# A product with stationary weights and 512 tokens moving, its sums turned in squares of 32 on VectorE

## The chip, the core and the metric

The kernel runs on one core of a Trainium2 chip. The metric is device time in microseconds of one execution. The engines of a core work side by side, each in the order of its own instruction list: PE (TensorE, matmuls; PEld is its weight load), DVE (VectorE), ACT (ScalarE), POOL (GpSimd); SP (SyncE) issues the DMAs. In a matmul one operand is stationary (loaded with LDWEIGHTS, 128x128) and the other moves past it column by column; the sums land in PSUM, eight banks of 128 partitions x 512 numbers. Compute engines read and write SBUF, 128 partitions.

## The reference

Chunked attention (batch 4, 8 heads, 768 tokens, head size 64) gives 3072 tokens x 512. Two feed-forward blocks follow:

```python
def _moe_ref(x, w1, w2, w3, w_out):
    h = np.maximum(np.maximum(x @ w1, x @ w2), x @ w3)      # 512 -> 768
    return (h @ w_out).astype(np.float32)                   # 768 -> 512

def _moe2_ref(x, w_in, w_out):
    h = x @ w_in                                            # 512 -> 2048
    g = np.where(h >= 1, h, np.where(h <= -1, 0.0, (h + 1) ** 2 / 4.0))
    return (g @ w_out).astype(np.float32)                   # 2048 -> 512
```

The change is in the last product, g @ w_out.

## The kernel before

All numbers are float32. A product is made of three fast matmuls: each operand is split into a rounded high half (float32r, made by ACT) and the rest (low half = value - high half, made by DVE or POOL), and high x high, high x low and low x high are added up in PSUM (`mm3`).

The first 500 us hold attention and the first feed-forward block, in 24 units of 128 tokens. Meanwhile the weights of the second block are prepared and put into DRAM in combinations (`cd` for w_in; `rd` and `td` for w_out). The second block then runs in three pairs of token blocks (2 x 512 tokens). A pair has two stages, and each of them multiplies 2 x 2 block matrices with seven block products in place of eight, in Winograd's form.

The stage on w_in, `pair_slot` for n = 0 to 7. Each n makes seven products of 128 features x 512 tokens, 6 matmuls of 512 columns each; the combined w_in is stationary and the combinations of x (`mat`, tiles t and b) move. Products go to the eight PSUM banks in turn. DVE adds them up to the four blocks h11, h12, h21 and h22 of the activations (feature x token); `g_start` (two ACT instructions) and `g_end` (one of DVE) apply the gate; `difference` (POOL) then replaces h21 by h11 - h21. Between products, `fill` splits the next w_in tile (`split_c`, ACT and POOL) or begins to split h for the next stage.

The stage on w_out, `pair_l4`: 56 steps, seven products k = 0 to 6 of eight steps. A step takes one tile of h (128 features x 512 tokens), split into hi and lo, and its w_out tile `w` (128 features x 256 outputs, `w[:, 0]` high, `w[:, 1]` low). For each 128 of the 512 tokens, three matmuls hold 128x128 of hi or lo and move the 256 columns of w: twelve matmuls a step into four banks (lines 820 to 822). In the same step `split_h(i + 4)` issues the split of the tile four steps ahead: ACT the high half (L746), DVE or POOL the low half (L748), DVE where the step number is in `ON_V`. The halves lie in nine buffers (`hb`) used in turn, so a low half's buffer is free when the step four before its own has been multiplied.

`evict` adds a finished product to the sums of the output blocks, one of the four banks (128 tokens x 256 outputs) in each of the next product's first four steps: two copies by ACT at first, otherwise adds by DVE, from PSUM into `outs`. A finished block is stored in rows of 256 numbers (`store_out`, L768).

`L4_STEPS` puts further work into the steps: L.. loads a half of a streamed w_out combination (`load_t`, into a buffer of `mat`; L30 is the first half for k = 3), S.. makes a combination of h blocks (`sum_h`, DVE, L764; two tiles at once, 1024 columns, or two times 512), X is the last `difference`, A to D load the four tiles of the next pair (`prep`, L646), T1 to T4 are their differences (DVE, L651), b11, t1 and so on split these (ACT L656, DVE L657), and c splits the first w_in tiles. The third pair has no successor and leaves A to t4 out. The order of every engine's list is the order of this code; nothing reorders it. SP waits at each DMA for what that one needs, and all later DMAs wait behind.

Of the kernel before, what the change touches and what calls it, by code (L numbers as in the profile page):

```python
# [19 lines left out]
P = 128  # L20
# [45 lines left out]
def attention_then_two_mlps(ctx, tc, q, k, v, mem_k, mem_v, w1, w2, w3, w_mid, w_in, w_out, out):  # L66
# [570 lines left out]
    SPOT = {"A": ("h11", 0), "B": ("h11", 1), "D": ("h11", 2), "C": ("h11", 3), "E": ("h21", 0)}  # L637
# [53 lines left out]
    def pair_slot(p, n, mid, fill):  # L691
# [3 lines left out]
        c21, c11, c12 = fb[0], fb[4], fb[5]  # L695
        h11, h12, h21, h22 = [h_tile(q, n) for q in ("h11", "h12", "h21", "h22")]
# [58 lines left out]
    def load_t(k, half):  # L755
        i = (2, 0, 1, 3)[k - 3]
# [3 lines left out]
    def sum_h(k, g):  # L760
        (o, a, b), op = {3: (("h11", "h22", "h11"), ALU.add), 5: (("h22", "h22", "h21"), ALU.subtract),
# [40 lines left out]

    outs = []

    def pair_l4(p, steps):

        for i in range(7 * HF):
            k, f = divmod(i, HF)
            if f == 0:
                done = cur.get("l4")  # L810
                cur["l4"] = acc4 = [next_bank() for _ in range(TB // P)]
# [5 lines left out]
            for t in range(TB // P):  # L817
                c = slice(t * P, (t + 1) * P)
                o = acc4[t][:, 0:HK]
                nc.tensor.matmul(o, hi[:, c], w[:, 0], start=f == 0, stop=False)  # L820
                nc.tensor.matmul(o, hi[:, c], w[:, 1], start=False, stop=False)  # L821
                nc.tensor.matmul(o, lo[:, c], w[:, 0], start=False, stop=f == HF - 1)  # L822
# [268 lines left out]
```

## Time and profile before

| | us |
|---|---|
| median of 3 runs | 1019.1 (1018.61 to 1019.78) |
| profiled execution | 1016.97 |
| its span, first to last instruction | 1015.2 |
| stages on w_in, pairs 2 and 3 | 77.50, 77.37 |
| stages on w_out, pairs 1, 2, 3 | 85.30, 84.75, 82.67 |

The rows below are from the profiled execution; times are from the start of its span. A stage is counted from the start of its first matmul to that of the next stage, the last one to the end of its last matmul. Rows of instructions name line, engine, operation and out<-in tiles without buffer numbers: hb is a half of a split, h a block of activations or a tile of the next pair, f a sum or a gate buffer, d, b and t weights of w_out or combinations of x. The granted clock of PE is 1.00 in all these stages, the higher of its two levels, 2.4 GHz.

### The profile page before, as it was taken

The numbers are of one execution on the slowest core, as the hardware profiler recorded it, in microseconds if no ns is written. First come the engines' busy times: TensorE is split into PE (matmuls) and PEld (weight loads), VectorE is DVE, ScalarE is ACT, GpSimd is POOL, SyncE is SP. The second block draws the span as 40 slices with busy tenths as digits, with TensorE's granted clock in tenths as the row PEclk, the third lists the DMA queues.
The fourth block names the chain that finished last, engine by engine and source line by source line (L and its number), as shares of the span: only waits on it lengthen the run. The fifth ranks groups of instructions, "written<-read, shape, count | busy, mean of one in ns | idle before, by whom it ended". The sixth has DMA issues, their size and how long they took to land.

```text
span 1015.2 us, 21316 instructions
## 1 busy us (share of the span) xinstructions
PE 983.1 (97%) x8262; PEld 832.7 (82%) x8262; DVE 725.5 (71%) x1096; ACT 521.9 (51%) x926; POOL 454.1 (45%) x368
## 2 busy tenths in 40 slices
PE   8999889999999999999999999999999999999998
PEld 6777677878788778788878889988889998888998
DVE  4699935567665776662337779898778988777974
ACT  5676434443234323322448775456786445786542
POOL 0024312222221011111647768487787667776754
PEclk9999999999999999999999999999999999999999
DMA  7857536667767576414323346313338033334421
GB/s 167 219 157 204 144 118 187 156 161 219 181 167 190 157 179 198 141 66 165 120 63 128 90 122 242 123 45 114 94 93 307 28 135 99 95 91 158 168 64 63
DMA packets 201781, 142.57 MB, mean 140 GB/s; under 512 B 128208, under 2 KB 169168, under 8 KB 201680
## 3 DMA queue, kind: packets, MB, share of 16 engines
q1 hardware_dynamic: 201680, 141.21, 47.8%
q8 instruction: 65, 1.06, 0.5%
q14 instruction: 36, 0.29, 0.1%
HBM read 109.71 MB, written 31.46 MB: 139 GB/s over the span
## 4 chain that ended last, share of the span: by engine, by line
PE 66%; DVE 12%; issue 6%; DMA 5%; ACT 4%; POOL 3%; SPq 3%; DVEq 0%; POOLq 0%; ACTq 0%
PE bank L502 14%; PE bank L503 14%; PE bank L504 14%; PE bank L822 6%; PE bank L820 6%; PE bank L821 6%; POOL hb L616 3%; SPq L846 2%; DVE c L145 2%; DVE c L150 1%; ACT f L678 1%; PE bank L373 1%; DVE c L142 1%; DMA st<-in_moe_w_dram 1%; PE bank L415 1%
## 5 line engine op out<-in xcount | busy, mean ns | idle before, releaser
L748 POOL TENSOR_TENSOR hb<-h,hb 128x512 fp32r<-128x512 f32 x96 | 165.6, 1737 | 78.2 <-PE bank L822 52.6
L502 PE MATMUL bank<-xh,hi 128*128 128x512 f32 x432 | 175.5, 406 | 1.2 <-ACT xh L443 0.7
L521 POOL TENSOR_TENSOR hl_a<-t,hh_a 128x512 fp32r<-128x512 f32 x34 | 47.5, 1396 | 281.6 <-ACT hh_a L519 222.1
L504 PE MATMUL bank<-xh,lo 128*128 128x512 f32 x432 | 169.3, 392 | 1.9 <-POOL lo L204 1.9
L503 PE MATMUL bank<-xl,hi 128*128 128x512 f32 x432 | 169.5, 392 | 0.3 <-DVE xl L447 0.2
L746 ACT CAST hb<-h 128x512 fp32r<-128x512 f32 x168 | 101.5, 621 | 90.4 <-PE bank L822 89.8
L537 DVE TENSOR_TENSOR t<-bank,t 128x512 f32<-128x512 f32 x72 | 49.4, 687 | 90.6 <-PE bank L504 90.3
L616 POOL TENSOR_TENSOR hb<-ra,hb 128x256 fp32r<-128x256 f32 x96 | 87.9, 933 | 28.8 <-ACT hb L615 23.3
L748 DVE TENSOR_TENSOR hb<-h,hb 128x512 fp32r<-128x512 f32 x72 | 87.0, 1218 | 18.1 <-PE bank L822 9.9
L504 PEld LDWEIGHTS bank<-xh,lo 128*128 128x128 f32 x432 | 81.4, 189 | 20.5 <-POOL lo L204 2.7
L502 PEld LDWEIGHTS bank<-xh,hi 128*128 128x128 f32 x432 | 81.6, 189 | 19.1 <-DVE t L537 1.0
L503 PEld LDWEIGHTS bank<-xl,hi 128*128 128x128 f32 x432 | 81.7, 189 | 16.1 <-DVE xl L447 1.0
L678 ACT ACTIVATE f<-h 128x512 f32<-128x512 f32 x96 | 60.8, 633 | 57.5 <-DVE h L713 35.2
L822 PE MATMUL bank<-d,hb 128*128 128x256 f32 x288 | 82.5, 287 | 3.6 <-POOL hb L748 2.8
L685 DVE SCALAR_TENSOR_TENSOR h<-f,h 128x512 f32<-128x512 f32 x96 | 78.8, 821 | 6.3 <-ACT f L679 6.0
L820 PE MATMUL bank<-d,hb 128*128 128x256 f32 x288 | 81.2, 282 | 0.0
L821 PE MATMUL bank<-d,hb 128*128 128x256 f32 x288 | 81.1, 282 | 0.0
L502 PE MATMUL bank<-t,hb 128*128 128x512 f32 x192 | 75.4, 393 | 0.9 <-ACT h L560 0.9
L504 PE MATMUL bank<-t,hb 128*128 128x512 f32 x192 | 75.5, 393 | 0.0
L503 PE MATMUL bank<-t,hb 128*128 128x512 f32 x192 | 75.4, 393 | 0.0
L204 POOL TENSOR_TENSOR lo<-c,hi 128x1024 fp32r<-128x1024 f32 x10 | 25.0, 2498 | 99.0 <-ACT hi L199 99.0
L616 POOL TENSOR_TENSOR hb<-rb,hb 128x256 fp32r<-128x256 f32 x72 | 59.7, 832 | 20.5 <-ACT hb L615 19.2
(146 smaller groups left out, 2541.7 us busy)
## 6 DMA issues: line engine op xcount, KB each, us to landing
ra<-cd SPq DMA_DIRECT2D x24, 512.0 KB
b<-td SPq DMA_DIRECT2D x12, 1024.0 KB
t<-td SPq DMA_DIRECT2D x12, 1024.0 KB
st<-in_moe_w_out_dram SPq DMA_DIRECT2D x22, 512.0 KB
st<-in_moe_w_dram SPq DMA_DIRECT2D x18, 512.0 KB
vw<-in_v_dram SPq DMA_DIRECT2D x152, 56.0 KB
st<-in_moe_w_in_dram SPq DMA_DIRECT2D x16, 512.0 KB
h<-yd SPq DMA_DIRECT2D x12, 512.0 KB
```

Of the source, the lines that this page charges most:

```text
L502: nc.tensor.matmul(out, whi, xhi, start=first, stop=False)
L503: nc.tensor.matmul(out, whi, xlo, start=False, stop=False)
L504: nc.tensor.matmul(out, wlo, xhi, start=False, stop=last)
L537: nc.vector.tensor_tensor(out=cur["t", j, f], in0=s, in1=cur["t", j, f], op=ALU.max)
L616: nc.gpsimd.tensor_tensor(out=c[:, 1], in0=t, in1=c[:, 0].bitcast(F32), op=ALU.subtract)
L678: nc.scalar.activation(out=a, in_=x, func=AF.Relu, bias=0.5, scale=0.5)
L685: nc.vector.scalar_tensor_tensor(out=x, in0=a, scalar=1.0, in1=x, op0=ALU.min, op1=ALU.max)
L746: nc.scalar.copy(out=hi, in_=x)
L748: e.tensor_tensor(out=lo, in0=x, in1=hi.bitcast(F32), op=ALU.subtract)
L820: nc.tensor.matmul(o, hi[:, c], w[:, 0], start=f == 0, stop=False)
L821: nc.tensor.matmul(o, hi[:, c], w[:, 1], start=False, stop=False)
L822: nc.tensor.matmul(o, lo[:, c], w[:, 0], start=False, stop=f == HF - 1)
```

## The change

The operands of the last product change sides: 128x128 of w is stationary and hi or lo moves, 512 tokens wide, six matmuls a step into two banks (outputs x tokens). `evict` adds whole banks of 512. A finished block is then outputs x tokens; `turned` transposes each square of 32x32 of it on DVE, and `store_out` writes it with four DMAs of 32 partitions, in runs of 32 numbers. The last product of the third pair is instead added in halves, turned on PE and copied by ACT (`last_evict`). The seven products come in another order (k = 0 takes h11, k = 1 h22; k = 3 takes h22 - h21 and k = 5 h11 + that), so blocks and buffers change places (A to D now lie in h22, by `SPOT`). At the end of a w_in stage (`early`) splits are issued ahead of the gates, and the last gate moves into the w_out stage.

```diff
-    SPOT = {"A": ("h11", 0), "B": ("h11", 1), "D": ("h11", 2), "C": ("h11", 3), "E": ("h21", 0)}
+    SPOT = {"A": ("h22", 0), "B": ("h22", 1), "D": ("h22", 2), "C": ("h22", 3), "E": ("h21", 0)}
...
+        early = n == HF - 1
...
         b = next_product(6)
         add(out=h21, in0=b, in1=c12)
-        g_start(h21)
+        if early:
+            fill()
+        else:
+            g_start(h21)
         g_end()
-        fill()
-
-    FACTORS = [("h22", 2), ("h11", 0), ("h12", 1), ("h11", "b22", "b11"), ("h21", "t2", "b21"), ("h22", "t3", "t1"),
+        if not early:
+            fill()
+
+    FACTORS = [("h11", 0), ("h22", 2), ("h12", 1), ("h22", "b11", "t4"), ("h21", "b21", "t3"), ("h11", "t1", "t2"),
                ("h12", "t4", "b22")]
-    LEAD, ON_V = 4, (2, *range(5, 40, 2), 42, 45, 47, 53, 55)
+    LEAD, ON_V = 4, (*range(1, 20, 2), 21, 24, 27, 30, 34, 37, 40, 43, 46, 49, 52, 55)
...
+    def store_out(p, i, d, x):
+
+        j, c = (2 * p + i) * TB, d * P
+        for r in range(0, P, CH):
+            nc.sync.dma_start(
+                out=out[j:j + TB, c + r:c + r + CH].rearrange("(t b) a -> b t a", b=CH),
+                in_=x[r:r + CH, :].rearrange("b (t a) -> b t a", a=CH))
+
+    def turned(p, i, d, t, x):
+        nc.vector.transpose(out=t.rearrange("p (t a) -> p t a", a=CH), in_=x.rearrange("p (t a) -> p t a", a=CH))
+        store_out(p, i, d, t)
+
+    def evict(p, k, f):
+
+        add = partial(nc.vector.tensor_tensor, op=ALU.add)
+        d = f % 2
+        x, one, two, u2 = extra[d], fb[d], fb[2 + d], fb[4 + d]
+        b = acc4[k][d]
+        if k == 0 and f < 2:
+            nc.scalar.copy(out=one, in_=b)
         elif k == 2:
-            add(out=c11, in1=x1)
+            if f < 2:
+                add(out=two, in0=b, in1=one)
+            else:
+                turned(p, 0, d, u2, two)
+        elif k == 3 and f < 2:
+            add(out=u2, in0=b, in1=one)
         elif k == 4:
+            if f < 2:
+                add(out=one, in0=b, in1=u2)
+            else:
+                add(out=two, in0=acc4[1][d], in1=one)
+                turned(p, 1, d, x, two)
         elif k == 5:
+            if f < 2:
+                add(out=u2, in0=b, in1=u2)
+                add(out=one, in0=b, in1=one)
+            else:
+                turned(p, 1, 2 + d, two, one)
+        elif k == 6 and f < 2:
+            add(out=u2, in0=b, in1=u2)
+            turned(p, 0, 2 + d, x, u2)
...
+    def last_evict(p):
+
+        for i in range(2):
+            z = acc4[0][i].rearrange("p (t c) -> p t c", t=2)
+            c = slice(i * HK, (i + 1) * HK)
+            for d in range(2):
+                u2 = fb[4 + d]
+                nc.vector.tensor_tensor(out=u2[:, c], in0=acc4[6][d][:, c], in1=u2[:, c], op=ALU.add)
+                for t in range(2):
+                    nc.tensor.transpose(z[:, t, d * P:(d + 1) * P], u2[:, (2 * i + t) * P:(2 * i + t + 1) * P], ident)
+            o = fb[i].rearrange("p (t c) -> p t c", t=2)
+            nc.scalar.copy(out=o, in_=z)
+            r0 = 2 * p * TB + 2 * i * P
+            nc.sync.dma_start(out=out[r0:r0 + 2 * P, HK:].rearrange("(t p) d -> p t d", p=P), in_=o)
...
+        def mms(k, f, w, hi, lo):
+            for d in range(2):
+                r = slice(d * P, (d + 1) * P)
+                mm3(acc4[k][d], w[:, 0, r], w[:, 1, r], hi, lo, f == 0, f == HF - 1)
...
-                cur["l4"] = acc4 = [next_bank() for _ in range(TB // P)]
+                acc4[k] = [banks[(base + (0, 2, 4, 6, 0, 4, 6)[k] + d) % 8] for d in range(2)]
...
+            mms(k, f, w, hi, lo)
             split_h(i + LEAD)
-            if k and f < TB // P:
-                evict(p, k - 1, f, done[f])
+            if i == 0:
+                g_start(h_tile("h21", HF - 1))
+            if k and f < 4:
+                evict(p, k - 1, f)
...
-        L4_STEPS = {0: "L30 L31 L40", 1: "L41 L50 L51 L60", 3: "X", 4: "S50", 6: "S51", 8: "S52", 10: "S53",
...
-                    28: "L61 A", 29: "B", 30: "D", 31: "C", 34: "b11", 36: "T1", 37: "T2",
...
+        L4_STEPS = {0: "L30 L31 L40", 1: "L41", 2: "X L50 L51 L61", 6: "S30", 8: "S31", 10: "S32", 13: "S33", 15: "S60", 17: "S50",
+                    18: "S61", 20: "S51", 21: "A", 22: "S62", 23: "S52 B", 25: "D", 26: "S63", 28: "S53 C", 29: "b11", 30: "T1",
+                    32: "L60", 33: "T2", 34: "T3", 36: "b21", 37: "T4", 40: "t3", 44: "t1", 48: "t2", 52: "t4 c",
...
```

The first step of the first pair's w_out stage on PE. Before (d is the w_out tile of k = 0, the banks hold 128 tokens each):

```order
L820 MATMUL bank_85<-d_0_5453,hb_5824 128x256
L821 MATMUL bank_85<-d_0_5453,hb_5824 128x256
L822 MATMUL bank_85<-d_0_5453,hb_5823 128x256
L820 MATMUL bank_86<-d_0_5453,hb_5824 128x256
L821 MATMUL bank_86<-d_0_5453,hb_5824 128x256
L822 MATMUL bank_86<-d_0_5453,hb_5823 128x256
L820 MATMUL bank_87<-d_0_5453,hb_5824 128x256
```

After:

```order
L502 MATMUL bank_85<-hb_5824,d_0_5531 128x512
L503 MATMUL bank_85<-hb_5823,d_0_5531 128x512
L504 MATMUL bank_85<-hb_5824,d_0_5531 128x512
L502 MATMUL bank_86<-hb_5824,d_0_5531 128x512
L503 MATMUL bank_86<-hb_5823,d_0_5531 128x512
L504 MATMUL bank_86<-hb_5824,d_0_5531 128x512
L502 MATMUL bank_85<-hb_5748,d_0_5531 128x512
```

The step has six matmuls where it had twelve; the seventh row is the next step's already. Lines 502 to 504 are those of `mm3`, which the w_in stage uses too.

DVE in the first pair's w_out stage, from the last sums of h on. Before, steps 27 to 36 (L748 low halves, L764 sums, L787 adds of an eviction, L657 a low half for the next pair, L651 its first difference):

```order
L764 TENSOR_TENSOR h_7_5738<-h_7_5738,h_3_5826 128x512
L748 TENSOR_TENSOR hb_5746<-h_0_5434,hb_5747 128x512
L748 TENSOR_TENSOR hb_5749<-h_1_5741,hb_5291 128x512
L787 TENSOR_TENSOR f_5285<-bank_81,f_5285 128x256
L748 TENSOR_TENSOR hb_5747<-h_2_5744,hb_5748 128x512
L787 TENSOR_TENSOR f_5285<-bank_82,f_5285 128x256
L787 TENSOR_TENSOR f_5286<-bank_83,f_5286 128x256
L657 TENSOR_TENSOR b_5400<-h_0_5310,b_5400 128x1024
L748 TENSOR_TENSOR hb_5291<-h_3_5825,hb_5290 128x512
L787 TENSOR_TENSOR f_5286<-bank_84,f_5286 128x256
L651 TENSOR_TENSOR h_1_5311<-h_1_5311,h_0_5310 128x1024
```

After, steps 26 to 33 (L759 low halves, L775 sums, L786 turns, L803 adds):

```order
L759 TENSOR_TENSOR hb_5291<-h_3_5328,hb_5290 128x512
L786 STREAM_TRANSPOSE f_5287<-f_5285 128x512
L775 TENSOR_TENSOR h_6_5737<-h_6_5737,h_3_5328 128x512
L775 TENSOR_TENSOR h_7_5738<-h_7_5738,h_3_5328 128x512
L786 STREAM_TRANSPOSE f_5288<-f_5286 128x512
L775 TENSOR_TENSOR h_3_5826<-h_3_5328,h_3_5826 128x1024
L657 TENSOR_TENSOR b_5400<-h_0_5310,b_5400 128x1024
L759 TENSOR_TENSOR hb_5290<-h_1_5741,hb_5289 128x512
L651 TENSOR_TENSOR h_1_5311<-h_1_5311,h_0_5310 128x1024
L803 TENSOR_TENSOR f_5287<-bank_83,f_5283 128x512
L759 TENSOR_TENSOR hb_5747<-h_2_5744,hb_5748 128x512
```

The sums of h now reach to step 28, and the work for the next pair begins at step 29 where it began at 34, so the two lie closer together, with low halves between them at every third step.

SP in the same stage. Before (L757 loads of w_out combinations, L646 the next pair's four tiles, L768 stores):

```order
L757 DMA t_5734<-td 128x4x512
L768 DMA out_dram<-f_5287 128x2x256
L768 DMA out_dram<-f_5288 128x2x256
L757 DMA b_5699<-td 128x4x512
L646 DMA h_0_5310<-yd 128x2x512
L646 DMA h_1_5311<-yd 128x2x512
L646 DMA h_2_5327<-yd 128x2x512
L646 DMA h_3_5328<-yd 128x2x512
```

After (L768 now the loads of w_out combinations, L781 the stores):

```order
L768 DMA b_5699<-td 128x4x512
L646 DMA h_0_5310<-yd 128x2x512
L646 DMA h_1_5311<-yd 128x2x512
L646 DMA h_2_5327<-yd 128x2x512
L781 DMA out_dram<-f_5287 32x16x32 x4
L781 DMA out_dram<-f_5288 32x16x32 x4
L646 DMA h_3_5328<-yd 128x2x512
L768 DMA t_5734<-td 128x4x512
```

Three of the next pair's four tiles are issued before the first stores, the fourth behind eight of them.

## Rows read from the trace of the kernel before

**Rows 1.** The page: busy time by engine; the chain that ended last, by engine

```profile
PE 983.1 (97%) x8262; PEld 832.7 (82%) x8262; DVE 725.5 (71%) x1096; ACT 521.9 (51%) x926; POOL 454.1 (45%) x368
...
PE 66%; DVE 12%; issue 6%; DMA 5%; ACT 4%; POOL 3%; SPq 3%; DVEq 0%; POOLq 0%; ACTq 0%
```

**Rows 2.** Windows: stretch, length, PE, PEld, DVE, ACT, POOL busy, clock, DMA share, GB/s

```profile
603.83:689.13 85.30, 82.42 (x674) 80.67 (x673) 78.44 (x87) 45.97 (x79) 59.59 (x34) 1.00 0.40 143
689.13:766.63 77.50, 77.50 (x338) 63.13 (x337) 59.70 (x88) 57.45 (x122) 57.72 (x63) 1.00 0.34 102
766.63:851.38 84.75, 81.90 (x673) 80.50 (x672) 78.11 (x85) 44.88 (x78) 60.59 (x35) 1.00 0.41 144
851.38:928.75 77.37, 77.37 (x338) 63.13 (x337) 59.54 (x88) 57.06 (x121) 55.50 (x62) 1.00 0.30 91
928.75:1011.42 82.67, 81.53 (x673) 80.34 (x671) 61.66 (x78) 37.87 (x67) 50.82 (x33) 1.00 0.35 122
976.95:999.85 22.90, 22.90 (x195) 22.90 (x194) 10.35 (x23) 9.98 (x16) 13.31 (x11) 1.00 0.18 50
...
621.16:644.55 23.39, 23.07 (x193) 22.80 (x192) 23.39 (x21) 11.32 (x21) 14.71 (x8) 1.00 0.17 61
```

**Rows 3.** Waits of PE, 603.83 to 1011.42: us in total, times, longest

```profile
PE bank L822 <- POOL hb L748: 5.1, 6, 1.2
PE bank L822 <- DVE hb L748: 1.6, 4, 0.5
```

**Rows 4.** Groups by form: busy us, mean ns | idle before, releaser

```profile
L748 POOL TENSOR_TENSOR hb<-h,hb 128x512 fp32r<-128x512 f32 x96 | 165.6, 1737 | 78.2 <-PE bank L822 52.6 <-ACT hb L746 23.7 <-POOL hb L748 1.3
L748 DVE TENSOR_TENSOR hb<-h,hb 128x512 fp32r<-128x512 f32 x72 | 87.0, 1218 | 18.1 <-PE bank L822 9.9 <-ACT hb L746 8.0 <-PE bank L821 0.2
L721 DVE TENSOR_TENSOR h<-bank,f 128x512 f32<-128x512 f32 x24 | 16.6, 691 | 14.7 <-PE bank L504 14.6
L401 PE MATMUL bank<-ident,p 128*128 128x128 f32 x96 | 14.7, 275 | 0.5 <-DVE xs L428 0.5
L405 ACT COPY aT<-bank 128x512 f32<-128x512 f32 x24 | 14.1, 586 | 55.1 <-PE bank L401 55.1
L351 DVE STREAM_TRANSPOSE kw<-kq 128x512 f32<-128x512 f32 x12 | 8.4, 704 | 17.6 <-DMA kq<-in_k_dram 12.4 <-DMA qs<-in_q_dram 5.2
L792 DVE TENSOR_TENSOR f<-bank,f 128x256 f32<-128x256 f32 x12 | 5.0, 414 | 3.3 <-PE bank L822 3.3
```

**Rows 5.** Timeline of DVE in the first w_out stage: start, us, instruction

```profile
621.16 1.21 DVE L764 TENSOR_TENSOR h<-h,h 128x1024 f32<-128x1024 f32 x1
622.29 1.78 DVE L748 TENSOR_TENSOR hb<-h,hb 128x512 fp32r<-128x512 f32 x1
...
638.29 0.68 DVE L748 TENSOR_TENSOR hb<-h,hb 128x512 fp32r<-128x512 f32 x1
638.88 0.41 DVE L781 TENSOR_TENSOR f<-bank,f 128x256 f32<-128x256 f32 x1
```

**Rows 6.** Timeline of POOL in the same stage, idle time before in brackets

```profile
608.09 1.27 POOL L748 TENSOR_TENSOR hb<-h,hb 128x512 fp32r<-128x512 f32 x1 [4.92 <-ACT hb L746]
...
621.24 2.28 POOL L748 TENSOR_TENSOR hb<-h,hb 128x512 fp32r<-128x512 f32 x1 [0.56 <-PE bank L822]
```

**Rows 7.** DMA queue, 302 to 307, loads in 128-byte runs: packets, MB, share

```profile
q1 hardware_dynamic: 3057, 0.38, 46.5%
```

**Rows 8.** DMA queue, 1011.4 to 1015.2: two stores in 1-KB runs, 512 data packets

```profile
q1 hardware_dynamic: 544, 0.52, 41.6%
```

**Rows 9.** Timeline of SP: eight loads of 48 KB in 128-byte runs

```profile
365.85 3.90 SPq L846 DMA_DIRECT2D kq<-in_k_dram  x8
```

**Rows 10.** Timeline of ACT: the first cast for the next pair

```profile
658.58 1.05 ACT L656 CAST b<-h 128x1024 fp32r<-128x1024 f32 x1 [3.14 <-DMA h<-yd]
```

**Rows 11.** Timeline of all engines, the end

```profile
1010.41 1.48 DVE L799 TENSOR_TENSOR f<-bank,f 128x256 f32<-128x256 f32 x4 [2.95 <-PE bank L822]
...
1011.14 0.28 PE L822 MATMUL bank<-b,hb 128*128 128x256 f32 x1
```

More of the change, by code (lines that the diff above doesn't have):

```diff
@@ L724, in pair_slot @@
         g_end()
-        fill()
+        if not early:
+            fill()
         b = next_product(5)
         add(out=h12, in0=b, in1=c21)
+        if early:
+            fill()
         g_start(h12)
         g_end()
-        fill()
+        if not early:
+            fill()
         b = next_product(6)
         add(out=h21, in0=b, in1=c12)
-        g_start(h21)
+        if early:
+            fill()
+        else:
+            g_start(h21)
         g_end()
-        fill()
-    FACTORS = [("h22", 2), ("h11", 0), ("h12", 1), ("h11", "b22", "b11"), ("h21", "t2", "b21"), ("h22", "t3", "t1"),
+        if not early:
+            fill()
+    FACTORS = [("h11", 0), ("h22", 2), ("h12", 1), ("h22", "b11", "t4"), ("h21", "b21", "t3"), ("h11", "t1", "t2"),
                ("h12", "t4", "b22")]
-    LEAD, ON_V = 4, (2, *range(5, 40, 2), 42, 45, 47, 53, 55)
+    LEAD, ON_V = 4, (*range(1, 20, 2), 21, 24, 27, 30, 34, 37, 40, 43, 46, 49, 52, 55)
     def split_h(i):
@@ L760, in sum_h @@
     def sum_h(k, g):
-        (o, a, b), op = {3: (("h11", "h22", "h11"), ALU.add), 5: (("h22", "h22", "h21"), ALU.subtract),
+        (o, a, b), op = {5: (("h11", "h22", "h11"), ALU.add), 3: (("h22", "h22", "h21"), ALU.subtract),
                          6: (("h12", "h12", "h22"), ALU.subtract)}[k]
@@ L807, in pair_l4 @@
+    def pair_l4(p, steps):
+        last = p + 1 == NB // 2
+        def mms(k, f, w, hi, lo):
+            for d in range(2):
+                r = slice(d * P, (d + 1) * P)
+                mm3(acc4[k][d], w[:, 0, r], w[:, 1, r], hi, lo, f == 0, f == HF - 1)
+        base = turn["bank"]
+        turn["bank"] += 2
         for i in range(7 * HF):
@@ L816, in pair_l4 @@
                 w = chunk_of(k, f)[:, f % 4]
[L817 to L822, printed above, removed]
+            mms(k, f, w, hi, lo)
             split_h(i + LEAD)
-            if k and f < TB // P:
-                evict(p, k - 1, f, done[f])
+            if i == 0:
+                g_start(h_tile("h21", HF - 1))
+            if k and f < 4:
+                evict(p, k - 1, f)
             for name in steps.get(i, "").split():
@@ L833, in pair_l4 @@
                 elif name == "X":
+                    g_end()
                     difference(HF - 1)
@@ L836, in pair_l4 @@
                     prep(p + 1, name)
-        for t in range(TB // P):
-            evict(p, 6, t, cur["l4"][t])
-        del cur["l4"]
+        if last:
+            last_evict(p)
+        else:
+            for f in range(2):
+                evict(p, 6, f)
     fetched, rounded, kept = [2 * Q1 + 4], [Q1], []
@@ L985, in attention_then_two_mlps @@
                     for g in (0, 1):
-                        hq["h11", g] = stage.tile([P, 2, TB], F32, tag="c", name=f"h11_{g}", bufs=2)
+                        hq["h22", g] = stage.tile([P, 2, TB], F32, tag="c", name=f"h22_{g}", bufs=2)
                 if t == 1:
                     for g in (2, 3):
-                        hq["h11", g] = w_tile(f"h11_{g}")
+                        hq["h22", g] = w_tile(f"h22_{g}")
                 for name in LAST_BLOCK.get(t, "").split():
@@ L1030, in last_l2 @@
             more_halves(1)
-            for q in ("h21", "h22"):
+            for q in ("h21", "h11"):
                 hq[q, 3] = w_tile(f"{q}_3")
@@ L1055, in attention_then_two_mlps @@
             if p == 0:
-                x = [hq["h21", 1][:, i].rearrange("p (t c) -> p t c", t=2) for i in range(2)]
-                outs.extend([[fb[2 * i + j].rearrange("p (t c) -> p t c", t=2) for j in range(2)] for i in range(3)] + [x])
+                extra.extend(h_tile("h21", 2 + i) for i in range(2))
             if p + 1 < NB // 2:
```

39 lines of the change are left out of this document (4 added, 35 removed), and 3 rows, old and new, of the table L4_STEPS.

## Prediction

> **What bounds the kernel now.** I read the page first: PE is busy 97% of the span and heads the chain of waits with 66%, DVE with 12% [rows 1]. Busy PE says little by itself, because the rows of pipelined matmuls overlap; so I cut the span into stages. The change touches only the last 411 us: three pairs of blocks, each with a stage on w_in and a stage on w_out. The stages on w_in last 77.50 and 77.37 us, those on w_out 85.30, 84.75 and 82.67 us [rows 2].
>
> Next, the pace of PE. A w_in stage issues 336 matmuls of 512 columns without a pause: 77.50 / 336 = 0.2307 us each. A w_out stage issues 56 x 12 = 672 matmuls of 256 columns. In the stretch 976.95 to 999.85, which has no pause, 16 steps or 192 matmuls take 22.90 us, 0.1193 us each [rows 2]. So the stage needs 672 x 0.1193 = 80.15 us of PE, and the rest, 5.15, 4.6 and 2.5 us, is waiting. The list of waits names it: PE waits for the low half of a split of h, from POOL 5.1 us and from DVE 1.6 us [rows 3]. The second matmul after a pause comes late too, which is most of the rest.
>
> Why those halves are late is the third reading. In a w_out stage DVE is busy 78.4 of 85.3 us [rows 2]. Its subtraction of two SBUF tiles takes 0.68 us alone (start to start 0.59) but 1.78 us beside POOL, and POOL's takes 1.27 alone (608.09) and 2.28 beside DVE (621.24) [rows 5, 6]. The two take turns: POOL's of 621.24 can only have begun when DVE's of 621.16 ended at 622.37, and ended at 623.52, a turn of 1.15 us; DVE's of 622.29 then ended 0.55 later. Turns are thus 0.60 us for DVE at 512 columns, 1.13 at 1024 (621.16 to 622.29) and 1.15 for POOL.
>
> **The change part by part.**
>
> PE. 672 matmuls of 256 columns become 336 of 512: 80.15 becomes 336 x 0.2307 = 77.5 us, 2.65 us less in each of three stages. The operands change sides, but the w_in stages already run 512 wide in the same three-matmul form, so I take their pace. Less is excluded, since they run it without a pause; at worst it is the old pace per column, 0.2386 us, and nothing is gained here.
>
> Evictions on DVE. Out go 36 adds of 256 columns at 0.414 us, 14.9 us a pair; in come 14 adds of 512 columns at 0.69 and 8 turns of 32x32 squares at 0.70 [rows 4]: 15.3 us. Nearly nothing is lost. None of them has two SBUF inputs, so POOL can run beside them. ACT loses eight short copies and gets two long ones.
>
> Splits. The list of those on DVE shrinks from 24 to 22 of 56; by the order, 20 of them lie inside the stage of the first pair, 23 or 24 before, and 32 on POOL, 30 or 31 before. DVE then has about 78.4 - 3 x 1.22 + 0.4 = 75.2 us of work for 77.5 us of PE.
>
> Turns. In the second pair's stage of before: DVE 24 x 0.60, ten sums of 1024 and four of 512 (13.7), four differences (4.5), six low halves for the next pair (6.8), three gates (1.8), together 41.2; POOL 31 x 1.15 + 1.15 + three small ones of 0.6 = 38.6. That is 79.8 of 84.75 us, 94%. Of after: DVE 38.8, POOL 39.8, together 78.6 us, against 77.5 of PE. So the stage of a pair with a successor cannot shrink to PE's time unless a little slips into the next w_in stage, where there is room.
>
> The place that decides is steps 13 to 35, where sums, transfers of the next pair and splits now lie together (the order of DVE shows it). After: DVE 8 splits, 7 sums of 1024, 4 of 512, one low half, 3 differences = 19.7; POOL 15 splits = 17.3; together 37 us in 23 steps of 1.384 = 31.8 us, 116%. Before, the same steps held 30.2 of 32.9 us, 92%. The slack: the buffer of the low half for step i+4 is free when step i ends, and it is read 0.23 us into step i+4: 3 x 1.384 + 0.23 = 4.4 us, less 1.15 for the subtraction itself, 3.2 us. 37 - 31.8 - 3.2 = 2.0 us of waiting if turns follow each other without a gap; if only 92% of the time can be filled, as then, 37 / 0.92 - 31.8 - 3.2 = 5.2 us. I take 2.5, nearer the first since that stretch of before had DVE busy for 23.39 of 23.39 us from 621.16 to 644.55 without stopping PE, and 0.5 us for the other places. The pauses at steps 3 and 4 of before (about 1.3 us) go: there POOL had waited 4.92 us for ACT's cast of its next split [rows 6], which stood behind the gates of the last w_in products; the change issues those casts ahead of the gates and puts the last gate into step 0. What is late next is the middle.
>
> The stage of pairs one and two: 77.5 + 3.0 = 80.5 us, gains of 4.8 and 4.25. The third has no successor, so no transfers, low halves or differences: in steps 13 to 35 the turns are 32.4 us against 31.8, within the slack. 77.66 us to the end of its last matmul plus 0.5 of pauses is 78.2, a gain of 4.5.
>
> DMA and SP. The first loads of a stage are as before. The stores of a pair were 8 of 256 KB; they become 32 of 64 KB, 512 runs of 128 bytes each. The trace has no write of such runs. Reads of them: 3057 packets in 5 us at a share of 46.5% of 16 engines, 12.2 ns a packet [rows 7]; writes of 1 KB: 41.6% of 16 x 3.8 us for 512 packets, 49 ns [rows 8]. A store takes 512 / 16 packets an engine, 0.4 us by the one and 1.6 us by the other. I take 0.4 to 0.8, near the reads of the same size. SP needs about 0.49 us for each [rows 9], 4 us for the eight of steps 26 and 27, and the load of the fourth tile of the next pair (step 28) now stands behind them. Before, DVE and ACT were held by the first such load for 3.14 us [rows 10]; now the first three are issued five to seven steps earlier, ahead of all stores. I count the queue at nothing, covered by DVE's own lateness of 3 to 5 us at that point; without that cover it costs up to 4 us a pair.
>
> The end. Before: the last matmul ends at 1011.42, the last add at 1010.41 + 1.48 = 1011.89, the span at 1015.2: 3.3 us from the last result to the end [rows 11]. After: the last half is added, turned on PE and copied by ACT. From the last matmul's start: 0.39 to its end and 0.05 for the signal, then three of four adds of 256 (the first is done by then), 0.41 + 2 x 0.34, to 1.53; two PE transposes of 0.28, ACT 0.59 [rows 4], signals 0.1, and 3.3 to the end: 6.1 us. Before it was 4.05. The end costs 2.0 us more.
>
> The boundary to the next w_in stage: DVE's last adds and turns run some 2 us longer into it; the next products have five of seven splits ready, so I count nothing.
>
> Sum: -4.8 - 4.25 - 4.5 + 2.0 = -11.55 us. The profiled execution took 1016.97 us, 1.8 more than its span, and the median of the runs is 2.1 above it at 1019.1. So 1005.4 by that execution's own time, 1007.5 by the median.
>
> **The rivals.**
>
> Nothing waits. Every pause goes: 77.66 us for each of the three, 7.6 + 7.1 + 5.0 - 2.0 = 17.7 us gained, 1001.5. For it: each split has four steps of lead, and before did not stop in a stretch with DVE full. Against it: 116%.
>
> DVE and POOL set the stage. If turns fill no more than 94% of a stage, as in the second pair of before, pairs one and two take 78.6 / 0.94 = 83.6 us, and the gain is 1.7 + 1.15 + 4.5 - 2.0 = 5.3 us: 1013.8. For it: rows 5 and 6. Against it: part of the 6% was the wait for a load. The Trainium skill (SBUF — State Buffer, "SBUF: two separate sides") says of these two engines that their common pair of ports is an exclusive lock held for a whole instruction; by that rule this rival's turns cannot overlap at all, and the turns of 0.6 and 1.15 us above agree with it.
>
> Short stores hold the queue: slower. At 49 ns for a packet of 128 bytes the eight stores of steps 26 and 27 take 12.5 us instead of 4. They leave from 41 us into the stage, so the fourth tile lands at about 55, while DVE comes to the difference that needs it at about 50; DVE stands there, and the split of step 40 behind it stops PE for about 3.5 us; at the end the stores of steps 50 and 51 overrun by 2.3 us. 2 x 3.5 + 2.3 = 9.3 us, which nearly eats the gain; from some 52 ns it is gone, and at 60 ns (6.4 us twice and 5.2) the kernel is 6.4 us slower than before, 1025.5. Against it: the reads at 12.2 ns. The Trainium skill (DMA: Bandwidth & Descriptors, "Specifications") says that transfers under 512 bytes are done as read-modify-write; it gives no price for it, and no run here shows a write that short.
>
> The wider form brings no pace. If 512 columns with w stationary go at 0.2386 us, PE needs 80.15 us; with the same 3.0 us of pauses the stages take 83.2, and the gain is 2.1 + 1.6 + 1.8 - 2.0 = 3.5: 1015.6. Against it: 1008 matmuls of that width in this trace.
>
> **How the numbers follow.** The forecast (1004 to 1011) 0.47, nothing waits 0.22, DVE and POOL 0.20, no pace 0.05, short stores 0.06. A change under 0.2%, 2 us, cannot be told from none here. Slower is the short stores' share, of which some would end within 2 us: 0.05; the same: 0.05, from those and the edges of the two small gains; faster 0.90. The range runs from the first rival's 1001.5, a little lower for pauses that I count at the end, to just past DVE and POOL's 1013.8: 1000.5 to 1014.5.
>
> **What would show it.** The three w_out stages at 80.5, 80.5 and 78.2 us, matmuls of 512 columns 0.231 us apart, no pause at steps 3 and 4, pauses for L759 between steps 20 and 40 of about 2.5 us in pairs one and two and hardly any in the third, the w_in stages unchanged, 6 us from the last matmul's start to the end. Stages of 83 us with DVE and POOL waiting on each other would show the second rival; a wait of the differences or of the adds for a DMA the third; a pace of 0.238 the last. I am wrong if the stages with a successor stay above 83 us or the end grows by over 4 us.

## The result: 0.6% slower, with the profile after

The changed kernel takes 1025.45 us (median of 18 runs, 1018.7 to 1028.55) against 1018.86 for the kernel before (18 runs): ratio 1.0062, 95% interval 1.0044 to 1.008. The forecast was 1007.5 us, in a range from 1000.5 to 1014.5. The profiled execution took 1024.2 us with a span of 1022.4.

By stages, profile after. Columns as in [rows 2]: stretch, length, then PE, PEld, DVE, ACT and POOL busy, granted clock, DMA share, GB/s.

```profile
606.62:691.96 85.34, 79.92 (x338) 63.90 (x336) 81.04 (x69) 44.18 (x72) 60.55 (x39) 0.98 0.42 129
691.96:769.51 77.55, 77.55 (x337) 63.13 (x336) 59.69 (x86) 56.52 (x120) 53.41 (x61) 1.00 0.37 103
769.51:856.06 86.55, 81.05 (x337) 63.52 (x336) 82.12 (x72) 45.06 (x73) 63.98 (x39) 0.98 0.46 140
856.06:933.46 77.40, 77.40 (x338) 63.12 (x336) 59.40 (x86) 56.47 (x120) 53.18 (x61) 1.00 0.37 107
933.46:1016.73 83.27, 80.53 (x339) 63.77 (x337) 62.15 (x63) 36.95 (x61) 53.61 (x34) 0.98 0.37 108
```

The w_in stages are as before; the w_out stages went from 85.30, 84.75 and 82.67 [rows 2] to 85.34, 86.55 and 83.27, where 80.5, 80.5 and 78.2 were forecast. PE needs less in them: between pauses its matmuls start 0.2307 us apart, 77.5 us a stage. It lost all of that again, by waiting and, for a few matmuls in each stage, by a slower clock. The list of PE's waits, 606.62 to 1016.6 (us in total, times, longest):

```profile
PE bank L503 <- DVE hb L759: 11.8, 7, 2.5
PE bank L503 <- POOL hb L759: 1.9, 4, 0.8
```

Before, POOL's halves were late for 5.1 us and DVE's for 1.6 [rows 3]; now it is DVE's. What DVE did ahead of one such pause, in step 27 of the third stage (start, us, instruction):

```profile
962.46 4.55 DVE L775 TENSOR_TENSOR h<-h,h 128x1024 f32<-128x1024 f32 x2
966.94 1.77 DVE L759 TENSOR_TENSOR hb<-h,hb 128x512 fp32r<-128x512 f32 x1
968.64 5.71 DVE L775 TENSOR_TENSOR h<-h,h 128x1024 f32<-128x1024 f32 x3
974.27 0.68 DVE L759 TENSOR_TENSOR hb<-h,hb 128x512 fp32r<-128x512 f32 x1
```

POOL at the same time:

```profile
962.04 3.90 POOL L759 TENSOR_TENSOR hb<-h,hb 128x512 fp32r<-128x512 f32 x2 [1.18 <-DVE h L775]
966.18 3.69 POOL L759 TENSOR_TENSOR hb<-h,hb 128x512 fp32r<-128x512 f32 x2 [0.25 <-issue]
970.33 3.47 POOL L759 TENSOR_TENSOR hb<-h,hb 128x512 fp32r<-128x512 f32 x2 [0.46 <-PE bank L504]
```

DVE never stops, and a sum of 1024 columns takes 2.3 us in the first row, 1.9 in the third, 1.21 where no turn of POOL's stands before it [rows 5]. The sums stand in front of the split, and PE behind it:

```profile
975.00 0.50 PE L503 MATMUL bank<-hb,b 128*128 128x512 f32 x1 [1.76 <-DVE hb L759]
...
976.39 0.63 PE L502 MATMUL bank<-hb,t 128*128 128x512 f32 x1
976.82 0.63 PE L503 MATMUL bank<-hb,t 128*128 128x512 f32 x1
```

The last two rows show a second loss: behind the pause the matmuls start 0.43 us apart instead of 0.23. The window over them (columns as above) has a granted clock of 0.53, with the edges of the stretch in it: the lower of the two levels, 1.2 GHz. Eight matmuls at 0.2 us more cost some 1.6 us, once in each stage: behind the pause of step 34 in the first, of step 27 in the others.

```profile
976.45:979.75 3.30, 3.30 (x10) 2.57 (x9) 3.30 (x6) 1.02 (x2) 1.71 (x2) 0.53 0.00 0
```

Sum in this pair of profiles: +0.04 + 1.80 + 0.60 for the stages and +1.9 from the last matmul's end to the end of the span (5.67 against 3.78 us), 4.3 us. The ratio stands for 4.5 to 8.2 us. The spans differ by 7.2: another 2.8 us lie ahead of the first w_out stage, which began at 603.83 before and at 606.62 after. That part is scatter between executions: in e2, below, whose code is that of the kernel before up to the first splits for this stage, the matmul 336 ahead of the stage started at 527.86 us, and in the kernel before at 524.99.

### The profile page after: what moved, and what is told of

Read it like the earlier page. It is cut to its first block, busy times and chain, and to the rows that moved or that the text cites. A ratio compares the mean times of both kernels' runs of the same rounds, so it can differ in the third digit from the quotient of the medians.

```text
span 1022.4 us, 19358 instructions
## 1 busy us (share of the span) xinstructions
PE 980.1 (96%) x7262; PEld 783.5 (77%) x7262; DVE 734.5 (72%) x1048; ACT 519.5 (51%) x910; POOL 454.9 (44%) x374
## 4 chain that ended last, share of the span: by engine, by line
PE 71%; DVE 14%; issue 5%; DMA 3%; SPq 3%; POOL 1%; ACT 1%; DVEq 0%; POOLq 0%; ACTq 0%
PE bank L503 22%; PE bank L502 22%; PE bank L504 22%; DVE hb L759 2%; DVE h L775 2%; DVE c L145 2%; DVE c L142 1%; DVE c L150 1%; PE bank L415 1%; PE bank L373 1%; DVE c L143 1%; SPq L261 1%; POOL hb L759 1%; SPq L886 1%; PE bank L435 1%
## 5 line engine op out<-in xcount | busy, mean ns | idle before, releaser
L759 POOL TENSOR_TENSOR hb<-h,hb 128x512 fp32r<-128x512 f32 x102 | 169.9, 1675 | 73.7 <-PE bank L504 42.3
L757 ACT CAST hb<-h 128x512 fp32r<-128x512 f32 x168 | 102.5, 619 | 114.0 <-PE bank L503 112.6
L616 POOL TENSOR_TENSOR hb<-ra,hb 128x256 fp32r<-128x256 f32 x96 | 85.9, 912 | 28.9 <-ACT hb L615 27.4
L759 DVE TENSOR_TENSOR hb<-h,hb 128x512 fp32r<-128x512 f32 x66 | 76.0, 1160 | 22.5 <-ACT hb L757 10.8
L678 ACT ACTIVATE f<-h 128x512 f32<-128x512 f32 x96 | 60.6, 632 | 53.4 <-DVE h L714 39.3
L775 DVE TENSOR_TENSOR h<-h,h 128x1024 f32<-128x1024 f32 (+1 forms) x42 | 75.6, 1822 | 4.2 <-POOL hb L759 3.5
L679 ACT ACTIVATE f<-f 128x512 f32<-128x512 f32 x96 | 60.8, 633 | 3.1
L503 PE MATMUL bank<-hb,d 128*128 128x512 f32 x144 | 57.5, 400 | 1.9 <-POOL hb L759 1.9
```

Of the source, the lines that this page charges most:

```text
L503: nc.tensor.matmul(out, whi, xlo, start=False, stop=False)
L616: nc.gpsimd.tensor_tensor(out=c[:, 1], in0=t, in1=c[:, 0].bitcast(F32), op=ALU.subtract)
L678: nc.scalar.activation(out=a, in_=x, func=AF.Relu, bias=0.5, scale=0.5)
L679: nc.scalar.activation(out=a, in_=a, func=AF.Square)
L757: nc.scalar.copy(out=hi, in_=x)
L759: e.tensor_tensor(out=lo, in0=x, in1=hi.bitcast(F32), op=ALU.subtract)
```

## The experiments

Theory: DVE and POOL take turns in their subtractions and sums, and so each split that POOL does makes DVE late. Rivals: DVE simply has too much work in the middle of the stage; the short stores hold it up. Each ratio is to the kernel before; the last column holds the three w_out stages of the profiled execution, counted as above.

| | edit | ratio | 95% interval | stages, us |
|---|---|---|---|---|
| | changed kernel | 1.0062 | 1.0044 to 1.008 | 85.34, 86.55, 83.27 |
| e1 | all splits on DVE | 0.9842 | 0.9806 to 0.9877 | 77.69, 78.30, 78.13 |
| e2 | before, all splits on DVE | 0.9994 | 0.9973 to 1.0014 | 83.01, 84.76, 84.97 |
| e3 | sums of h spread later | 1.0046 | 1.0027 to 1.0064 | 86.22, 88.63, 79.25 |
| e4 | stores in runs of 1 KB | 1.0051 | 1.0025 to 1.0078 | 84.85, 87.44, 83.21 |
| e5 | a third of the splits on POOL | 0.9935 | 0.9918 to 0.9952 | 81.70, 83.54, 81.09 |
| e6 | e1 and unused work on POOL | 1.0509 | 1.0486 to 1.0532 | 103.33, 104.38, 93.1 |
| e7 | e1, gates in the old order | 0.9971 | 0.9956 to 0.9987 | 81.08, 82.38, 82.66 |
| e8 | before, e1's splits, new gate order | 0.9899 | 0.9876 to 0.9923 | 80.08, 81.44, 80.56 |
| e9 | before, new gate order | 0.9977 | 0.9958 to 0.9995 | 84.25, 84.61, 81.98 |

**e1.** The changed kernel with no split on POOL in the w_out stages. (In a diff or a profile, ... stands for lines not shown.)

```diff
-    LEAD, ON_V = 4, (*range(1, 20, 2), 21, 24, 27, 30, 34, 37, 40, 43, 46, 49, 52, 55)
+    LEAD, ON_V = 4, range(56)
```

> The changed kernel with all 56 low halves of a w_out stage subtracted on VectorE, none on GpSimd. Theory (the pauses of PE come from turns at the shared port, where each of VectorE's sums of 1024 columns takes 2.3 us instead of 1.13 because GpSimd's subtractions of 1.15 us stand between): VectorE alone has 56 x 0.6 + 13.7 + 4.5 + 6.8 + 15.3 = 74 us for 77.5 us of PE; the pause at step 27 goes, VectorE's sums take 1.2 us in the rows, the stages fall from 85.3, 86.6 and 83.1 to 78 to 81, and the kernel takes 1000 to 1012 us, ratio to the kernel before 0.982 to 0.994. Rival 1 (VectorE simply has too much work in the middle of the stage, whoever shares the port): it gets 34 more subtractions, so the pauses grow and the stages stay at 86 or more, ratio over 1.006. Rival 2 (the short stores hold VectorE or the queue): stages as they are, ratio 1.004 to 1.008.

One line takes off 2.2%: 1003.87 us, the fastest kernel of this study, as the theory had it; of 21.6 us between the medians, the three stages of the profiles hold 21.0. The pause at step 27 is gone. DVE has 34 more splits a stage and is busy for less time. The first lines of the two pages, changed kernel:

```profile
PE 980.1 (96%) x7262; PEld 783.5 (77%) x7262; DVE 734.5 (72%) x1048; ACT 519.5 (51%) x910; POOL 454.9 (44%) x374
```

and e1:

```profile
PE 969.8 (97%) x7262; PEld 779.6 (78%) x7262; DVE 723.1 (72%) x1150; ACT 518.8 (52%) x910; POOL 288.8 (29%) x272
```

102 instructions more, 11 us less. The groups by form say why (busy us, mean ns). The second stage of the changed kernel:

```profile
L759 DVE TENSOR_TENSOR hb<-h,hb 128x512 fp32r<-128x512 f32 x22 | 27.9, 1278 | 3.3 <-ACT hb L757 3.1
L775 DVE TENSOR_TENSOR h<-h,h 128x1024 f32<-128x1024 f32 x10 | 19.2, 1924 | 1.4 <-POOL hb L759 1.2
L651 DVE TENSOR_TENSOR h<-h,h 128x1024 f32<-128x1024 f32 x4 | 7.5, 1865 | 0.1
L657 DVE TENSOR_TENSOR t<-h,t 128x1024 fp32r<-128x1024 f32 x4 | 6.9, 1717 | 0.0
L775 DVE TENSOR_TENSOR h<-h,h 128x512 f32<-128x512 f32 x4 | 5.8, 1489 | 0.0
```

and of e1:

```profile
L759 DVE TENSOR_TENSOR hb<-h,hb 128x512 fp32r<-128x512 f32 x55 | 37.7, 705 | 2.5 <-PE bank L504 1.4 <-ACT hb L757 0.7 <-issue 0.3
L775 DVE TENSOR_TENSOR h<-h,h 128x1024 f32<-128x1024 f32 x10 | 12.2, 1216 | 0.0
L651 DVE TENSOR_TENSOR h<-h,h 128x1024 f32<-128x1024 f32 x4 | 4.9, 1225 | 0.0
L657 DVE TENSOR_TENSOR t<-h,t 128x1024 fp32r<-128x1024 f32 x4 | 4.9, 1214 | 0.0
...
L775 DVE TENSOR_TENSOR h<-h,h 128x512 f32<-128x512 f32 x4 | 2.5, 676 | 0.0
```

Against the lengths of e1, the 22 splits of the changed kernel are 12.6 us longer in all, the sums 7.1 and 3.3, and of the work for the next pair four differences (L651) and four splits (L657) 4.6: 27.5 us, 0.83 for each of POOL's 33 splits. On DVE such a split takes 0.60 from start to start. Handing one to POOL thus takes 0.6 us off DVE and puts 0.8 on. The Trainium skill (Perfetto Trace Analysis, "Optimizing Scalar/DVE Operations") says that moving work between these two "might not help", since they share a port; here it cost 2.2%.

**e6.** Do the two engines take turns, or do DVE's sums wait for POOL's results? Here POOL does work beside e1 that nobody reads. (The edit is shown against the changed kernel, whose list of splits also becomes that of e1.)

```diff
+    unused = []
...
-            e = nc.vector if i in ON_V else nc.gpsimd
-            e.tensor_tensor(out=lo, in0=x, in1=hi.bitcast(F32), op=ALU.subtract)
+            nc.vector.tensor_tensor(out=lo, in0=x, in1=hi.bitcast(F32), op=ALU.subtract)
+            if i not in (*range(1, 20, 2), 21, 24, 27, 30, 34, 37, 40, 43, 46, 49, 52, 55):
...
+                nc.gpsimd.tensor_tensor(out=unused[0], in0=x[:, 0:448], in1=hi[:, 0:448].bitcast(F32), op=ALU.subtract)
```

> The kernel with all splits on VectorE, plus 34 subtractions of 448 columns on GpSimd in each w_out stage, at the places where the changed kernel has its own, from the same operands into a tile that nobody reads. Nothing depends on them but the buffer of the high half. Theory (the two engines take turns at a common port): VectorE's sums of 1024 columns again take about 2.2 us instead of 1.22, its splits over 1.2 instead of 0.70, it is busy 75 + 33 x 0.8 = 100 us of work in a stage of 77.5, so the stages grow to 90 to 105 us and the kernel to 1040 to 1085 us, ratio 1.02 to 1.065. Rival (VectorE was late because its sums and splits depended on GpSimd's late results): nothing depends on these, so stages stay at 78, ratio 0.982 to 0.988.

1071.15 us, in the theory's range. In the second stage DVE has 56 splits and the same sums as in e1, and POOL 33 subtractions (its row is the last):

```profile
L759 DVE TENSOR_TENSOR hb<-h,hb 128x512 fp32r<-128x512 f32 x56 | 61.1, 1119 | 1.9 <-ACT hb L758 1.9
L779 DVE TENSOR_TENSOR h<-h,h 128x1024 f32<-128x1024 f32 x10 | 15.0, 1499 | 0.0
```

```profile
L763 POOL TENSOR_TENSOR unused<-h,hb 128x448 fp32r<-128x448 f32 x33 | 48.9, 1482 | 43.9 <-ACT hb L758 43.1
```

The window of this stage, then of e1's (columns as above):

```profile
791.29:895.67 104.38, 85.34 (x338) 60.66 (x336) 104.31 (x107) 45.21 (x73) 54.96 (x39) 1.00 0.37 115
```

```profile
758.01:836.31 78.30, 77.79 (x338) 62.95 (x336) 75.41 (x105) 44.81 (x73) 5.84 (x5) 1.00 0.50 153
```

DVE is busy 104.31 us here and 75.41 there: 28.9 us for 33 instructions that give it nothing, 0.88 each. Its sums grew less than expected (1.50 us, not 2.2), its splits nearly as much (1.12, not 1.2). What DVE loses is thus a matter of the two engines' access, not of waiting for results. The Trainium skill (SBUF — State Buffer, "SBUF: two separate sides") calls the pair of ports of these engines an exclusive lock for a whole instruction; the rows agree: in the changed kernel a sum took up to 2.3 us, its own turn of 1.13 and POOL's of 1.15.

**e5.** How the loss grows with the number of splits on POOL.

```diff
-    LEAD, ON_V = 4, range(56)
+    LEAD, ON_V = 4, [i for i in range(56) if i % 3 != 2]
```

> The changed kernel with every third split (i mod 3 = 2, 18 of 56) on GpSimd and 38 on VectorE: a point between none (ratio 0.9842) and 34 (1.006). In the second w_out stage of the changed kernel VectorE was busy 82.1 us with 33 splits on GpSimd, and 75.4 with none; without its own 33 splits it should have been 75.4 - 33 x 0.69 = 52.6, so each split on GpSimd made VectorE's other rows 29.5 / 33 = 0.89 us longer and took 0.69 off. Theory (turns at the port): VectorE is busy about 75.4 + 18 x 0.2 = 79 us in the second stage, over PE's 77.5; pauses of 1 to 4 us a stage, ratio 0.987 to 0.996, slower than with none on GpSimd. Rival (only VectorE's own share counts and 34 on GpSimd was merely too many): VectorE's load falls to about 63 us, no pause at all, ratio 0.984 or lower.

0.9935, as the theory said. The second stage:

```profile
765.71:849.25 83.54, 79.83 (x338) 62.39 (x337) 80.38 (x87) 44.95 (x73) 32.87 (x23) 1.00 0.47 143
```

DVE's busy time in this stage is 75.41 us with none on POOL, 80.38 with 18 and 82.12 with 33, although each of them is one instruction less on DVE. PE's longest pause in the three stages is 1.2 us; all its lost time comes to 4.2, 6.0 and 3.4 us a stage, more than the 1 to 4 us expected.

**e3.** Is it the crowding at steps 15 to 23, or what the whole stage holds?

```diff
-        L4_STEPS = {0: "L30 L31 L40", 1: "L41", 2: "X L50 L51 L61", 6: "S30", 8: "S31", 10: "S32", 13: "S33", 15: "S60", 17: "S50",
-                    18: "S61", 20: "S51", 21: "A", 22: "S62", 23: "S52 B", 25: "D", 26: "S63", 28: "S53 C", 29: "b11", 30: "T1",
...
+        L4_STEPS = {0: "L30 L31 L40", 1: "L41", 2: "X L50 L51 L61", 8: "S30", 11: "S31", 14: "S32", 17: "S33", 20: "S50",
+                    22: "S60", 24: "A", 25: "S51", 27: "S61", 28: "B", 30: "S52", 31: "b11", 32: "S62 L60", 33: "D T1",
...
```

> The changed kernel with the twelve sums of h spread over steps 8 to 36 instead of 6 to 28, and the differences and low halves for the next pair moved behind them (to steps 24 to 55); the number of instructions is the same. Theory (the pause at step 27 comes from seven sums and four small splits crowded into steps 15 to 23): the pause at step 27 and the eight slow matmuls behind it go, about 3.4 us in each stage, while those at steps 34 to 49 may grow by part of it since the whole stage is 94% to 100% full; ratio 1.002 down to 0.994 (1012 to 1020 us), the third stage at 79 to 80. Rival (the stage's whole content decides, not its order): the pauses move but their sum stays at 8 to 9 us, ratio 1.004 to 1.008, the third stage still at 82 to 83.

Both, each in its stage; the ratio, 1.0046, is the rival's and lies outside the theory's 0.994 to 1.002, and the third stage is the theory's. This stage, which has no work for a next pair, came down from 83.27 to 79.25 and lost its pause at step 27 and the slow matmuls: there crowding was the cause. In the first two the pause at step 27 went as well, but others of up to 2.0 us at steps 37 to 43 and of 3.0 and 4.3 us at step 49 took its place, and both stages got longer: there what DVE and POOL have to do did not fit in either of the two orders. The kernel as a whole gained nothing that can be told (1.0046 against 1.0062).

**e4.** The stores: as many, from the same tiles and of the same size, but in runs of 1 KB, which put the squares in other places of the output.

```diff
-        j, c = (2 * p + i) * TB, d * P
+        j, c = (2 * p + i) * TB + d % 2 * HK, d // 2 * HK
...
-                out=out[j:j + TB, c + r:c + r + CH].rearrange("(t b) a -> b t a", b=CH),
-                in_=x[r:r + CH, :].rearrange("b (t a) -> b t a", a=CH))
+                out=out[j + 2 * r:j + 2 * r + 2 * CH, c:c + HK].rearrange("(b t) a -> b t a", t=2),
+                in_=x[r:r + CH, :].rearrange("b (t a) -> b t a", a=HK))
```

> The changed kernel with its 32 stores of a pair made of runs of 1 KB instead of 128 bytes: as many DMAs, as many bytes, from the same tiles, but the squares land in wrong places of the output. Theory (turns at the port and crowding; stores are hidden): within 1 us of the changed kernel, ratio 1.004 to 1.008, stages and pauses as they are, except for up to 0.5 us at the pauses behind step 30. Rival (short stores hold the queue or the memory port): stages one and two shorter by 2 us or more each, ratio under 1.002.

No difference that can be told (1.0051 against 1.0062). The changed kernel's own trace also gives the price that no row of before had. Queue over 677.8 to 683, eight stores of 128-byte runs (packets, MB, share of 16 engines):

```profile
q1 hardware_dynamic: 4224, 0.52, 58.9%
```

0.589 x 16 x 5.2 / 4224 = 11.6 ns a packet, beside 12.2 for the reads [rows 7], 0.37 us a store.

**e2, e7, e8, e9.** The kernel before with all splits on DVE (e2), then the new order of the gates taken out of e1 (e7), put into e2 (e8) and put into the kernel before alone (e9). The edit of e2:

```diff
-    LEAD, ON_V = 4, (2, *range(5, 40, 2), 42, 45, 47, 53, 55)
+    LEAD, ON_V = 4, range(56)
```

of e7, against e1 (e8 and e9 make the reverse of it in the kernel before, where the last `difference` also moves from step 3 to step 2):

```diff
-        early = n == HF - 1
+        early = False
...
-            if i == 0:
-                g_start(h_tile("h21", HF - 1))
...
-                    g_end()
```

> The kernel before, with the same single edit: all 56 low halves of a w_out stage on VectorE. Separates the wide product from the division of the splits. Theory (turns at the port): its pauses go too, and its stages come down from 85.3, 84.8 and 82.7 to its PE time of 80.15 plus about 1 us; ratio 0.988 to 0.996, some 4 to 6 us slower than the changed kernel with this edit. Rival (VectorE is the bound by its own work): stages over 86, ratio over 1.005.

> The kernel with all splits on VectorE, and the fills (ScalarE's copies of the first splits) of the last w_in slot again behind the gates, the last gate in that slot, as in the kernel before. Theory (this order alone made the pauses at steps 2 to 5): pauses of 3 to 4.7 us at steps 2 to 5 of each stage, as the kernel before with all splits on VectorE has them, PE waiting on ScalarE's copies; ratio 0.9842 + 11 / 1020 = 0.992 to 0.997. Rival (with 512 columns the copies have time enough): pauses under 1.5 us, ratio 0.983 to 0.988.

> The kernel before (256-column products) with both of the other edits: all splits on VectorE, and the first splits' copies ahead of the last gates. Against the kernel with all splits on VectorE and 512-column products it lacks only the wide product. Theory (each edit does its own share): PE's 672 x 0.1193 = 80.15 us a stage and 0.3 to 1 us of pauses, so stages of 80.4 to 81.2; against 77.7, 78.3 and 78.0 that is 3 x 2.7 = 8 us, less the 2.0 us that its end is shorter, 6 us: ratio 0.9842 + 0.006 = 0.988 to 0.992. Rival (the wide product also loads VectorE and the queues less or more than its PE time says): ratio outside 0.986 to 0.994.

> The kernel before with the new order of the gates alone; 31 or 32 splits on GpSimd as they were. Theory: its pauses at steps 3 and 4 (1.4 us a stage, 1.5 in the third) go, those at steps 23 to 47 (2.5 us) stay, so it gains 3 to 5 us: ratio 0.995 to 0.998. Rival (the time given back at the start is used up by VectorE and GpSimd at their port, as in the changed kernel): pauses at steps 23 to 47 grow by as much, ratio 0.999 to 1.002.

e2 missed: 0.9994, where 0.988 to 0.996 was expected. Its late pauses did go, but 2.9 to 4.75 us of new ones a stage came at steps 2 to 5. ACT there, around the second stage's start (a row's bracket: idle before, and what ended it):

```profile
768.21 0.63 ACT L678 ACTIVATE f<-h 128x512 f32<-128x512 f32 x1 [2.11 <-DVE h L721]
...
769.41 0.61 ACT L746 CAST hb<-h 128x512 fp32r<-128x512 f32 x1
771.45 0.63 ACT L678 ACTIVATE f<-h 128x512 f32<-128x512 f32 x1 [1.43 <-DVE h L727]
...
772.65 0.60 ACT L746 CAST hb<-h 128x512 fp32r<-128x512 f32 x1
```

and DVE:

```profile
770.12 0.69 DVE L748 TENSOR_TENSOR hb<-h,hb 128x512 fp32r<-128x512 f32 x1 [0.75 <-ACT hb L746]
770.73 0.68 DVE L727 TENSOR_TENSOR h<-bank,f 128x512 f32<-128x512 f32 x1
...
773.35 0.69 DVE L748 TENSOR_TENSOR hb<-h,hb 128x512 fp32r<-128x512 f32 x1 [1.34 <-ACT hb L746]
```

A ring: DVE's split waits for ACT's copy (L746), DVE's next add (L727) stands behind that split, ACT's gate (L678) waits for the add, and the next copy stands behind the gate. One copy per turn, 3.2 us, while PE wants one every 1.43, a step of twelve matmuls. A split on POOL stands in another engine's list, and the add does not wait behind it. The new gate order takes the copies out of the ring. e7 puts the ring back, and comes out at the slow edge of what was expected, 0.9971 where 0.992 to 0.997 was: PE waits for ACT's copies 5.7 us in all, and the stages are 3.4 to 4.5 us longer than in e1, 1.3% in the ratio. With neither the ring nor splits on POOL, e8 runs the kernel before at PE's pace in the first stage, 80.08 us, and up to 1.3 us above it in the others; its ratio is the theory's. e9 is at the upper end of what was expected: the pauses at step 3 went, but pauses of 0.6 to 0.7 us came at step 8.

## Why the prediction was wrong

PE's pace was right, 0.2307 us. What the wide product itself is worth shows where nothing else holds it: e1 is 0.57% of the time before, 5.8 us, under e8, with 6 expected from the pace and the end. The intervals of the two ratios all but touch, which leaves this some 4 us either way; the stages of the profiles less the longer end give 6.1. The stores (11.6 ns) and the w_in stages were right, and so was the end. The last matmul after:

```profile
1016.33 0.40 PE L504 MATMUL bank<-hb,b 128*128 128x512 f32 x1
```

From its start to the end of the span, 1022.4, it is 6.07 us, where 6.1 was forecast and 4.05 was the time before [rows 11]. SP issued eight stores in 4.11 us, near the 3.90 of [rows 9]:

```profile
677.85 4.11 SPq L781 DMA_DIRECT2D out_dram<-h  x8
```

The step that failed is the sum of turns: "37 - 31.8 - 3.2 = 2.0 us of waiting if turns follow each other without a gap", and "75.2 us of work" for DVE before it. The pauses were forecast at 3.0, 3.0 and 0.5 us; the stages less PE's 77.5 (77.66) show 7.8, 9.05 and 5.6, and that is the whole miss: 4.8, 6.05 and 5.1 us of the 16 between -11.55 and +4.3. By the prediction's own sign, stages with a successor above 83 us, it was wrong. The middle, steps 13 to 35, lost 6.4, 4.3 and 4.0 us, slow matmuls included, where 2.5, 2.5 and nothing was forecast and even the 5.2 us that was set aside would not have covered the first stage. The rest of each stage lost 1.4, 4.8 and 1.6 us, where 0.5 was forecast: there were also pauses of 1.4 us at step 49 of pair one, and of 0.9, 1.7 and 1.4 us at steps 4, 40 and 49 of pair two. Three errors are in it:

- DVE's work was carried over at its length from before (78.4 less three splits of 1.22). But these lengths hold waits for POOL, and they grew: the sums of 1024 from 1.77 to 1.92 us in the second stage, those of 512 from 0.95 to 1.49. DVE got fewer splits, and its busy time there went from 78.1 to 82.1 us; in the first stage, for which 75.2 was forecast, it is 81.0. The sums of before in that stage, to be read beside those of the changed kernel above:

```profile
L764 DVE TENSOR_TENSOR h<-h,h 128x1024 f32<-128x1024 f32 x10 | 17.6, 1766 | 0.0
...
L764 DVE TENSOR_TENSOR h<-h,h 128x512 f32<-128x512 f32 x4 | 3.7, 952 | 0.0
```

In turns, 78.6 us filled 92% of 85.34 and 91% of 86.55, the filling of before's middle that I set aside for 100%. Nor had the turns fallen, from 79.8 to 78.6 us: counted by the rows that start inside the stage, at the same prices, they are 78.7 us in each of these two stages before and 80.4 and 81.0 after, because POOL has two more splits and two more small ones of the next w_in tile there, and DVE no more than three splits less. That is 92 to 93% of the stage before and 94% after.
- The slack of 3.2 us was spent once on an average over steps 13 to 35. In the third stage, where that average lies within it, the sums ahead of the split of step 27 still stopped PE; spread out (e3) they did not.
- A pause can cost twice, by the slower clock behind it: three pauses of 1.9 to 2.6 us (beyond the usual 0.23 from start to start) did, at some 1.6 us each. No pause of before was longer than 1.4 us, none had this behind it, and the sum has no such term.

Of the rivals, "DVE and POOL set the stage" had the cause and, at 83.6 us a stage, came nearest for pairs one and two; it took the third for free. "Nothing waits" gave 1001.5: what e1 reaches, 1003.87, once POOL is out of it. The new gate order is worth more than the 1.3 us a stage that I gave it only without POOL's splits: 1.3% there, 4 us a stage, but 0.23% in the kernel before, 0.8 us a stage; in the changed kernel itself pauses of 0.9 and 1.0 us at step 4 stayed in the second and third stage. In the kernel before, part of the waits for turns hid behind a slower PE; the change sped up an engine that did not set the length of the stage.

## What to carry to other kernels

Before work on two SBUF tiles is handed from VectorE to GpSimd, compare what it frees (the instruction's start-to-start time) with what GpSimd's instruction adds to VectorE's others: take their lengths with and without GpSimd beside them from the rows. Half of a row that is twice its undisturbed length is waiting, and work for an engine must be counted at the undisturbed length plus the other engine's turns. When the bounding engine is sped up, look first at which engine would set the stage next, and try the cheapest shift of its load (here one list) before and after.

## Not expected of the hardware

- Around some pauses of PE the granted clock fell to its lower level, and the 8 to 12 matmuls behind them started 0.43 us apart at 512 columns. In the changed kernel, e3 and e4, 7 of the 11 pauses of 1.9 us or more had this behind them, and no shorter one did; three of 1.9 us and one of 3.0 us did not, and in e6 only one of five such pauses did. What decides stays open.
- The turn of a tile of 512 columns in squares of 32x32 took 0.70 us on DVE, in the changed kernel and in e1 alike; it has one input in SBUF, and POOL beside it did not lengthen it.
